# A gated linear-attention block: late division loads queued behind the second left side, first operands of the second layer asked for earlier

## The chip, the core and the metric

The kernel runs on one core of a Trainium2 chip. The metric is the device time of one execution in microseconds (us), as the median of several runs. The engines are named as in the profile: PE (matrix multiply), PEld (its weight loads), DVE (vector), ACT (scalar), POOL (GpSimd), SP (which here only issues transfers). POOL issues transfers too.

## What is computed

The reference, cut to what matters (S = 2048 tokens, D = 1024, F = 3584, 32 heads of 32, all float32):

```python
xn  = layernorm(x)
q, k, v = heads(xn @ wqkv)                    # phi(t) = where(t > 0, t + 1, exp(t)) + 1e-6
kv  = einsum("bhsd,bhse->bhde", phi(k), v);  z = sum over s of phi(k)
s   = (phi(q) @ kv) / (phi(q) . z + 1e-6) @ wo
g   = silu((silu(xn @ w1) * (xn @ w3)) @ w2)
out = x + s * g
```

## The kernel before, in words

Every large product is done by a Strassen-like scheme of seven products (`PRODUCTS`, L65: B11, T2, T3, T1, B21, T4, B22, each with its partner on the left: A11, S2, S3, S1, A12, A22, S4). Every operand is split into a high and a low part (`split`, L79: a cast on ACT at L83, then a subtraction on DVE at L84), and a product is three matmuls on those parts (`mm3`, L88: L91, L92, L93).

The first half of the program (two calls of `half`, L762) makes q, k, v and the gated hidden layer. Small side jobs run between its products: `catch_up` (L323) advances one job by one step and orders what the step issues behind marks, the copy and the addition just traced. The ordering call adds an order only between instructions of the same engine. A job that is queued with True is also ordered behind the load kept in the list `fetched` (L263), which is issued by SP; one queued with False is not.

Then comes **attention** (L967 to L973): eight groups of tokens, m = 0 to 7, 256 tokens each. The right side is the merged output weight: seven groups `wpr` of 1 MB each, loaded by two transfers each (L957) into two rotating `raw` buffers, split into tiles `wp` and kept for all tokens. The left side of a group of tokens is seven loads (`left`, L890) from `qs_d`, split into X tiles; those of m = 0 land in `job` buffers, the others in the four `sg` buffers. m = 0 is "outer": all seven products are built at once, step by step along the contraction (28 products of 3 matmuls), so that it can start while the right side is still coming. The others run one product after another, 84 matmuls each, with a `catch_up` after six of the seven.

`qs_d` is written by **divisions** (`divide`, L679): two loads of denominators (L688) and two of queries (L690), a multiplication on DVE (L696), four sums on POOL and a store (L699). There are four divisions for each m. Those for m = 6 and 7 are "late": the job of L764, whose steps run in the catch-ups of attention tokens 1 and on. It loads two divisions at its first step and one more after each finished one; a division has three empty steps before its multiplication. The `job` buffers are three.

The **second layer** (L974 to the end) multiplies the hidden layer by w2 in five segments; the first has 2 steps of contraction, the others 3. Its left side is again seven loads (L890, from `h_d` and `hs_d`), its right side `second_weights` (L905: a load at L907 into one of the six `c` buffers, which the attention's results s also use until they are stored), split into tiles of the pool `pw` (L974). `pw` takes the memory that the pools of the first part (`era1`: pa, praw, st, in that order, L100 to L102) give back at L973: its first tiles lie on the first of those pools, which is `pa`, where the attention's right side is. A tile waits for the tiles that lay at its addresses. In tracing order the second layer asks first for the left side of its tokens 0 (L984) and then for the right side (L985).

The program text gives the tracing order; a scheduler places the instructions on the engines' queues by that priority, by its own estimate of when each can run, and by free buffers. Each engine then works its queue in order.

Of the kernel before, what the change touches and what calls it, by code (L numbers as in the profile page):

```python
# [9 lines left out]
F32 = mybir.dt.float32  # L10
# [6 lines left out]
P = 128  # L17
C = 512
# [4 lines left out]
def tile_linear_attention_times_swiglu(  # L23
# [10 lines left out]
    nc = tc.nc  # L34
    x, out = x[0], out[0]
# [29 lines left out]
    PRODUCTS = ["B11", "T2", "T3", "T1", "B21", "T4", "B22"]  # L65
# [31 lines left out]
    pe = ctx.enter_context(tc.tile_pool(name="pe", bufs=3))  # L97
    pc = ctx.enter_context(tc.tile_pool(name="pc", bufs=6))
    era1 = ExitStack()
    pa = era1.enter_context(tc.tile_pool(name="pa", bufs=1))  # L100
    praw = era1.enter_context(tc.tile_pool(name="praw", bufs=2))
    st = era1.enter_context(tc.tile_pool(name="st", bufs=2))  # L102

    kvacc = st.tile([P, ND, P], F32, tag="kvacc", bufs=1, name="kvacc")
    nc.vector.memset(kvacc, 0.0)
# [1 line left out]
    def small(name):  # L107
        return pc.tile([P, C], F32, tag="c", name=name)

    def signed(name):  # L110
        return pc.tile([P, C], F32, tag="sg", bufs=4, name=name)

    def job_tile(shape, name):
        return praw.tile(shape, F32, tag="job", bufs=3, name=name)

    def load_rows(rows, name):

# [51 lines left out]
    def load_second(mom, g):  # L169

        ts = []
        for i in (2 * g, 2 * g + 1):
            ts.append(job_tile([P, D], f"xb{i}") if i < 3 else pb.tile([P, D], F32, tag="b", name=f"xb{i}"))
            nc.sync.dma_start(out=ts[-1], in_=x[C + i * P:C + (i + 1) * P, :])
        j = TH // 2 + 2 * g
        moments(ts, mom[:, j:j + 2])
        return ts
# [21 lines left out]
    def prepare_next(i):  # L199
# [12 lines left out]

        def steps(_):
            t = [job_tile([P, D], f"xn{i}_{e}") for e in range(2)]
            for c in range(2):
                r0 = HS + c * C + i * P
# [49 lines left out]
    fetched = []  # L266
# [54 lines left out]
    jobs = []  # L321
# [262 lines left out]
    def weight_sums(u, half):  # L584

        cols = slice(half * 2 * P, (half + 1) * 2 * P)

        def load():
            t = job_tile([P, 4, 2 * P], f"w2_{u}_{half}")
            for e in range(2):  # L590
                f = 2 * u + e
                nc.sync.dma_start(out=t[:, 2 * e:2 * e + 2],
                                  in_=w2[f * P:(f + 1) * P, :].rearrange("p (n c) -> p n c", c=C)[:, :, cols])
            return t

        def steps(t):
            yield True
            yield from sums_of(*(t[:, i] for i in range(4)))
            yield True
            nc.sync.dma_start(out=wt_d[u][:, :, cols], in_=t)  # L600
            yield True

        return Job(load, steps)
# [32 lines left out]
    def go_on(work):  # L636

        data = [j.load() for j in work[:2]]
        for i, j in enumerate(work):
            yield from j.steps(data[i])  # L640
            if i + 2 < len(work):
                data.append(work[i + 2].load())
# [36 lines left out]
    def divide(m, k):  # L679

        c, cols = m // NT, slice(m % NT * 2 * P, (m % NT + 1) * 2 * P)

        def load():
            t = job_tile([P, 4, 2 * P], f"qd{m}_{k}")
            for e in range(2):
                j = k + e * (ND // 2)
                rows = r_d[c][j * (P // DH):(j + 1) * (P // DH), cols]
                nc.sync.dma_start(out=t[:, 2 + e], in_=bass.AP(  # L688
                    tensor=rows.tensor, offset=rows.offset, ap=[[C, P // DH], [0, DH], [1, 2 * P]]))
                nc.sync.dma_start(out=t[:, e], in_=pq_d[j // JG][c][:, j % JG, cols])  # L690
            return t

        def steps(t):
            for _ in range(3):
                yield True
            nc.vector.scalar_tensor_tensor(t[:, :2], t[:, :2], 1e-6, t[:, 2:], op0=ALU.add, op1=ALU.mult)  # L696
            for _ in four_sums(t[:, 0], t[:, 1], t[:, 2], t[:, 3]):
                pass
            nc.gpsimd.dma_start(out=qs_d[m][:, k], in_=t)  # L699
            divided.add((m, k))  # L700
            yield True

        return Job(load, steps)
# [45 lines left out]
    def late_work():  # L749
        yield from go_on([divide(m, k) for m in range(LATE, S // (2 * P)) for k in range(ND // 2)])  # L750
# [10 lines left out]

    for h in range(NH):  # L762
        half(h)
    jobs.append((late_work(), False))  # L764


    GT = 2 * P
# [2 lines left out]
    class Segment:  # L770


        def __init__(self, name, nk, first, place, right, left, acc, end=None):
            self.name, self.nk, self.first = name, nk, first
            self.place, self.right_of, self.left_of, self.acc, self.end = place, right, left, acc, end
            self.Y, self.X = {}, {}
# [97 lines left out]
    def left(m, g, halves, sums, nk, name, first=False):  # L874

        halves = [t.rearrange("p k (g t s) -> p k g t s", t=2, s=P) for t in halves]
        sums = [t.rearrange("p k (n g s) -> p k n g s", n=2, s=P) for t in sums]
        where = {"A11": halves[0][:, :, g, 0], "A12": halves[1][:, :, g, 0], "A22": halves[1][:, :, g, 1]}
        for n in range(4):
            where[f"S{n + 1}"] = sums[n // 2][:, :, n % 2, g]  # L880
        big = None
        for e, n in enumerate(PRODUCTS):
            n = PARTNER[n]
            if first:
                if e % 2 == 0:
                    big = job_tile([P, 2, nk, P], f"r{e}{name}_{m}")
                t = big[:, e % 2]
            else:
                t = signed(f"r{n}{name}_{m}")[:, :nk * P].rearrange("p (k s) -> p k s", s=P)
            nc.sync.dma_start(out=t, in_=where[n])  # L890
            yield n, t

    def queries(m):
        while any((m, k) not in divided for k in range(ND // 2)):
            next(jobs[0][0])
        q = qs_d[m]
        return left(m, 0, [q[:, :, e] for e in range(2)], [q[:, :, 2 + e] for e in range(2)], ND // 2, "q", m == 0)

    def hiddens(i, m):
        h_ = h_d[i][m // NT].rearrange("p (k e) s -> p k e s", e=2)  # L900
        hs = hs_d[i][m // NT]
        return left(m, m % NT, [h_[:, :, e] for e in range(2)], [hs[:, :, e] for e in range(2)],
                    (FB[i][1] - FB[i][0]) // 2, f"B{i}")

    def second_weights(i, n, k):  # L905
        t = small(f"r{n}B{i}_{k}")
        nc.sync.dma_start(out=t, in_=second_weight(i, n, k))  # L907
        return t

    def second_weight(i, n, k):  # L910
        f0, f1 = FB[i]
        if n[0] == "T":
            return wt_d[f0 // 2 + k][:, ["T1", "T3", "T4", "T2"].index(n)]
        f = f0 + 2 * k + int(n[1]) - 1
        o = (int(n[2]) - 1) * C
        return w2[f * P:(f + 1) * P, o:o + C]
# [11 lines left out]
        nc.vector.tensor_add(a, a, xs)  # L928
        nc.gpsimd.dma_start(out=out[r0:r0 + P, cols], in_=a)

    def run(seg, nxt=None, around=None):

        def between(k):
            if m == NG - 1 and nxt:
                if k == 0:
                    nxt.operands(0)
                    for e in range(seg.nk, nxt.nk):
                        nxt.right(e)
                if k < nxt.nk:
                    nxt.right(k)  # L940

        if not seg.X:
            seg.operands(0)
        for m in range(NG):
            if m + 1 < NG:
                seg.operands(m + 1)
            seg.tokens(m, m == 0 or m == NG - 1 and nxt is not None, between)


# [11 lines left out]
    def attention_place(n, i, k):  # L961
# [3 lines left out]
    attention = Segment("s", ND // 2, True, attention_place,  # L965
                        attention_right, queries, lambda m, t, n: small(f"s{m}_{t}{n}"), store_s)
    attention.operands(0)  # L967
    for k in range(attention.nk):
        attention.right(k)
    run(attention)  # L970
    assert all(next(j, None) is None for j, _ in jobs)
    jobs.clear()
    era1.close()  # L973
# [2 lines left out]
    def layer_place(n, i, k):  # L976
        return pw.tile([P, 2, C], FR, tag=f"{n}_{k}", name=f"{n}_{k}")

    acc = []
    layers = [Segment(f"B{i}", (f1 - f0) // 2, i == 0, layer_place, lambda n, _, k, i=i: second_weights(i, n, k),  # L980
                      lambda m, i=i: hiddens(i, m), lambda m, t, n: acc[m][:, t, n],
                      finish if i == len(FB) - 1 else None)
              for i, (f0, f1) in enumerate(FB)]
    layers[0].operands(0)  # L984
    for k in range(layers[0].nk):  # L985
        layers[0].right(k)
    acc.extend(pw.tile([P, 2, 2, C], F32, tag=f"acc{m}", name=f"acc{m}") for m in range(NG))
    for i, seg in enumerate(layers):
# [24 lines left out]
```

## Time and profile before

| what | us |
|---|---|
| median of 3 runs | 2445.79 (2444.87 to 2446.43) |
| the profiled execution, its own time | 2438.58 |
| its span, first to last instruction | 2436.8 |
| PE busy | 2344.2 (96%) |
| DVE, ACT, POOL busy | 1810.3, 928.0, 723.7 |
| granted PE clock, mean | 0.992 |

The clock is given as a share of the full 2.4 GHz. A line of a timeline gives the start, the duration, the engine, the source line, the operation, what it writes and reads, how many instructions were merged, and in brackets how long the engine was idle before it and who released it.

### The profile page before, as it was taken

To read this page: it belongs to the slowest core of one execution; us is meant where nothing else is said; L and a number is where in the kernel's file an instruction comes from. 1 tells how busy PE (TensorE), PEld (TensorE's weight loads), DVE (VectorE), ACT (ScalarE), POOL (GpSimd) and SP (SyncE) were. 2 spreads that over 40 slices of the span, in tenths; PEclk is the share of its full clock that TensorE was granted. 3 is DMA by queue.
4 is the path that set the end of the run, shared out by engine and by line. 5 is a ranking of instruction groups with operands and counts; after the bars stand their busy time and mean duration, and the time that the engine had idled before them with its cause. 6 is when DMAs were issued, how large, how long until landed. Compare 5 with 4: busy or idle time off the path is not lost.

```text
span 2436.8 us, 30795 instructions
## 1 busy us (share of the span) xinstructions
PE 2344.2 (96%) x10544; PEld 1927.2 (79%) x10544; DVE 1810.3 (74%) x2688; ACT 928.0 (38%) x1663; POOL 723.7 (30%) x909
## 2 busy tenths in 40 slices
PE   6999989999999999999999999999899999999987
PEld 5788777778888888888778888888687887778776
DVE  8645788888887764657888887888655767776797
ACT  4434544332333233445433323333323434343443
POOL 3000021465554310000343543244330032323253
PEclk9999999999999999999999999999999999999999
DMA  4221555665555581124455556457776545454587
GB/s 139 70 69 45 172 168 171 220 212 196 184 203 178 184 290 35 52 83 144 163 192 180 191 191 207 136 187 243 242 234 194 152 130 157 120 163 116 169 288 240
DMA packets 375133, 408.62 MB, mean 168 GB/s; under 512 B 19840, under 2 KB 308608, under 8 KB 374976
## 3 DMA queue, kind: packets, MB, share of 16 engines
q1 hardware_dynamic: 348800, 319.35, 41.9%
q0 software_dynamic: 26176, 87.31, 9.5%
q8 instruction: 82, 1.34, 0.2%
q14 instruction: 75, 0.61, 0.1%
HBM read 268.96 MB, written 137.63 MB: 167 GB/s over the span
## 4 chain that ended last, share of the span: by engine, by line
PE 75%; DVE 11%; DMA 6%; issue 5%; ACT 1%; POOL 1%; SPq 0%; DVEq 0%; POOLq 0%; ACTq 0%
PE dB L93 1%; PE kv L442 1%; PE cB L91 1%; PE dB L91 1%; PE dB L92 1%; PE cB L93 1%; PE cB L92 1%; PE aB L93 1%; PE aB L91 1%; PE aB L92 1%; DMA wpr<-wp_d 1%; PE trk L409 1%; PE trv L409 1%; DMA rA11B<-h_d 1%; PE cs L93 1%
## 5 line engine op out<-in xcount | busy, mean ns | idle before, releaser
L511 POOL DMA_DIRECT2D pq_d<-pq x32 | 17.5, 548 | 501.2 <-DVE pq L403 461.6
L564 POOL DMA_DIRECT2D h_d<-sg x112 | 62.0, 553 | 331.1 <-DVE sg L563 320.6
L849 POOL TENSOR_TENSOR acc<-acc,uB 128x512 f32<-128x512 f32 x25 | 41.9, 1676 | 157.8 <-DVE uB L846 157.8
L546 POOL TENSOR_TENSOR qd<-qd 128x128 f32<-128x128 f32 x32 | 25.4, 795 | 129.1 <-DVE qd L696 121.1
L578 POOL TENSOR_TENSOR w<-w 128x256 f32<-128x256 f32 x28 | 26.4, 944 | 106.7 <-DMA w<-in_B_w 106.5
L826 POOL TENSOR_TENSOR acc<-acc,uB 128x512 f32<-128x512 f32 x7 | 10.9, 1560 | 149.3 <-ACT uB L818 149.3
L410 ACT ACTIVATE kvr<-trk 128x512 f32<-128x512 f32 x32 | 19.1, 597 | 88.0 <-PE trk L409 84.8
L550 POOL TENSOR_TENSOR hs<-sg,hs 128x256 f32<-128x256 f32 x56 | 51.9, 927 | 1.7
L547 POOL TENSOR_TENSOR hs<-hs,sg 128x256 f32<-128x256 f32 x56 | 46.5, 830 | 0.0
L919 POOL DMA_DIRECT2D s_d<-s x32 | 17.5, 546 | 92.9 <-DVE s L856 41.6
L546 POOL TENSOR_TENSOR hs<-sg,sg 128x256 f32<-128x256 f32 x56 | 42.1, 751 | 1.0
L91 PE MATMUL cB<-T,XA22B 128*128 128x512 f32 x87 | 35.0, 403 | 7.3 <-DVE acc L853 7.0
L549 POOL TENSOR_TENSOR hs<-sg 128x256 f32<-128x256 f32 x56 | 41.5, 740 | 0.0
L83 ACT CAST XS4B<-rS4B 128x384 fp32r<-128x384 f32 (+1 forms) x40 | 19.6, 490 | 54.0 <-PE cB L93 44.6
L851 POOL TENSOR_TENSOR acc<-acc,uB 128x512 f32<-128x512 f32 x25 | 40.0, 1600 | 0.0
L84 DVE TENSOR_TENSOR XS1B<-rS1B,XS1B 128x384 fp32r<-128x384 f32 (+1 forms) x40 | 36.4, 910 | 4.1 <-ACT XS1B L83 4.0
L867 DVE TENSOR_TENSOR acc<-cB,acc 128x512 f32<-128x512 f32 x25 | 17.2, 688 | 29.7 <-PE cB L93 29.7
L83 ACT CAST XS1B<-rS1B 128x384 fp32r<-128x384 f32 (+1 forms) x40 | 19.7, 493 | 48.5 <-PE cB L93 26.2
L926 ACT ACTIVATE acc<-acc 128x512 f32<-128x512 f32 x32 | 20.2, 632 | 46.3 <-DVE acc L856 14.1
L83 ACT CAST XA11B<-rA11B 128x384 fp32r<-128x384 f32 (+1 forms) x40 | 19.7, 493 | 44.9 <-PE dB L93 28.4
L83 ACT CAST XS3B<-rS3B 128x384 fp32r<-128x384 f32 (+1 forms) x40 | 19.7, 491 | 43.3 <-DMA rS3B<-hs_d 20.5
L91 PE MATMUL aB<-B,XA12B 128*128 128x512 f32 x87 | 34.1, 392 | 1.9 <-ACT uB L843 1.9
(5861 smaller groups left out, 8899.6 us busy)
## 6 DMA issues: line engine op xcount, KB each, us to landing
h_d<-sg POOLq DMA_DIRECT2D x112, 256.0 KB, 3.1
qs_d<-qd POOLq DMA_DIRECT2D x32, 512.0 KB, 4.1
hs_d<-hs POOLq DMA_DIRECT2D x60, 256.0 KB, 3.5
w<-in_B_w SPq DMA_DIRECT2D x56, 256.0 KB
wt_d<-w SPq DMA_DIRECT2D x28, 512.0 KB
hs_d<-hs SPq DMA_DIRECT2D x52, 256.0 KB
pq_d<-pq POOLq DMA_DIRECT2D x32, 256.0 KB, 3.0
pqd<-pq_d SPq DMA_DIRECT2D x16, 512.0 KB
```

Of the source, the lines that this page charges most:

```text
L83: nc.scalar.copy(out=hi, in_=src)
L91: nc.tensor.matmul(acc, lhsT=wh, rhs=ah, start=start, stop=False, skip_group_check=True)
L92: nc.tensor.matmul(acc, lhsT=wh, rhs=al, start=False, stop=False, skip_group_check=True)
L93: nc.tensor.matmul(acc, lhsT=wl, rhs=ah, start=False, stop=stop, skip_group_check=True)
L409: nc.tensor.transpose(p_[:, t * P:(t + 1) * P], src[:, t * P:(t + 1) * P], ident)
L546: nc.gpsimd.tensor_add(out=s1, in0=a21, in1=a22)
L547: nc.gpsimd.tensor_sub(out=s2, in0=s1, in1=a11)
L549: nc.gpsimd.tensor_sub(out=s3, in0=a11, in1=a21)
L550: nc.gpsimd.tensor_sub(out=s4, in0=a12, in1=s2)
L564: nc.gpsimd.dma_start(out=h_d[i][2 * h + c][:, 2 * k + n], in_=sg[n, c])
L849: G.tensor_add(out=c22, in0=c22, in1=u)
L851: G.tensor_add(out=c12, in0=c12, in1=u)
```

## The change

- The order in which the pools of the first part are opened is now st, pjob, praw, pa; the `job` buffers get a pool of their own (same number and size).
- The late divisions are queued with True, and `fetched` is set to the load just issued by `left` for attention tokens 0 and 1. So what SP issues for them in a catch-up is ordered behind the last left-side load of tokens 1.
- Ahead of the last attention tokens (m = 7), `ask_first` issues the loads of the second layer's B11, T2, T3 and T1 for contraction step 0, the first two into buffers of the pool `pe` (tag u, three buffers), the others into `c` buffers. `second_weights` uses them when it finds them.
- The first right side (k = 0) is traced ahead of the left side of tokens 0.

```diff
     era1 = ExitStack()
+    st = era1.enter_context(tc.tile_pool(name="st", bufs=2))
+    pjob = era1.enter_context(tc.tile_pool(name="pjob", bufs=3))
+    praw = era1.enter_context(tc.tile_pool(name="praw", bufs=2))
     pa = era1.enter_context(tc.tile_pool(name="pa", bufs=1))
-    praw = era1.enter_context(tc.tile_pool(name="praw", bufs=2))
-    st = era1.enter_context(tc.tile_pool(name="st", bufs=2))
...
-        return praw.tile(shape, F32, tag="job", bufs=3, name=name)
+        return pjob.tile(shape, F32, tag="job", name=name)
...
-    jobs.append((late_work(), False))
+    jobs.append((late_work(), True))
...
-            nc.sync.dma_start(out=t, in_=where[n])
+            load = nc.sync.dma_start(out=t, in_=where[n])
+            if name == "q" and m < 2:
+                fetched[:] = [load]
...
+    asked = {}
+    def ask(i, n, k, place):
+        asked[i, n, k] = t = place(f"r{n}B{i}_{k}")
+        nc.sync.dma_start(out=t, in_=second_weight(i, n, k))
     def second_weights(i, n, k):
-        t = small(f"r{n}B{i}_{k}")
-        nc.sync.dma_start(out=t, in_=second_weight(i, n, k))
-        return t
+        if (i, n, k) not in asked:
+            ask(i, n, k, small)
+        return asked[i, n, k]
+    def spare(name):
+        return pe.tile([P, C], F32, tag="u", name=name)
+    def ask_first():
+        for n, place in zip(PRODUCTS, (spare, spare, small, small)):
+            ask(0, n, 0, place)
...
             if m + 1 < NG:
                 seg.operands(m + 1)
+            elif ahead:
+                ahead()
...
-    run(attention)
+    run(attention, ahead=ask_first)
...
+    layers[0].right(0)
     layers[0].operands(0)
-    for k in range(layers[0].nk):
+    for k in range(1, layers[0].nk):
         layers[0].right(k)
```

## Rows read from the trace of the kernel before

**Rows 1.** The page, busy us of each engine, share of the span, instructions

```profile
PE 2344.2 (96%) x10544; PEld 1927.2 (79%) x10544; DVE 1810.3 (74%) x2688; ACT 928.0 (38%) x1663; POOL 723.7 (30%) x909
```

**Rows 2.** Stretches: us, busy (count) PE PEld DVE ACT POOL, clock, DMA share, GB/s

```profile
1704.90:1725.20 20.30, 11.91 (x31) 7.36 (x31) 10.21 (x15) 6.70 (x12) 6.13 (x9) 0.75 0.72 233
...
1745.20:1858.50 113.30, 113.30 (x501) 93.63 (x499) 55.23 (x85) 27.47 (x48) 32.20 (x59) 1.00 0.64 203
1858.50:1868.00 9.50, 5.52 (x13) 3.89 (x13) 5.16 (x8) 4.24 (x8) 0.54 (x1) 0.64 0.97 296
1868.00:1880.00 12.00, 12.00 (x53) 9.57 (x52) 9.53 (x17) 9.53 (x19) 0.00 (x0) 1.00 0.88 276
1880.00:1896.00 16.00, 14.54 (x59) 10.49 (x58) 15.59 (x32) 6.76 (x16) 0.00 (x0) 1.00 0.71 215
```

**Rows 3.** Who PE waited for: us in total, times, longest

```profile
PE T1s L91 <- ACT wp L83: 5.4, 1, 5.4
...
PE B11B L91 <- ACT B L83: 2.9, 1, 2.9
```

**Rows 4.** Timeline of SP, start of attention (merged issues)

```profile
1693.49 0.83 SPq L957 DMA_DIRECT2D wpr<-wp_d  x2
1694.69 0.57 SPq L688 DMA_DIRECT2D qd<-r_d  x1
...
1698.41 2.05 SPq L957 DMA_DIRECT2D wpr<-wp_d  x2
...
1707.50 0.53 SPq L688 DMA_DIRECT2D qd<-r_d  x1
1708.89 1.52 SPq L957 DMA_DIRECT2D wpr<-wp_d  x2
...
1728.38 0.52 SPq L890 DMA_DIRECT2D rS4q<-qs_d  x1
```

**Rows 5.** Transfers issued and moved from 1693 to 1721

```profile
DMA packets 5478, 8.46 MB, mean 302 GB/s; under 512 B 434, under 2 KB 4057, under 8 KB 5478
...
qd<-r_d SPq DMA_DIRECT2D x6, 128.0 KB
qd<-pq_d SPq DMA_DIRECT2D x6, 128.0 KB
```

**Rows 6.** Timelines of ACT, DVE and POOL, the right side's last groups

```profile
1699.27 1.14 ACT L83 CAST wp<-wpr 128x512 fp32r<-128x512 f32 x2 [1.45 <-DMA wpr<-wp_d]
...
1719.74 1.14 ACT L83 CAST wp<-wpr 128x512 fp32r<-128x512 f32 x2 [8.51 <-DMA wpr<-wp_d]
...
1699.93 4.39 DVE L84 TENSOR_TENSOR wp<-wpr,wp 128x512 fp32r<-128x512 f32 x2 [0.77 <-ACT wp L83]
...
1704.84 1.28 DVE L84 TENSOR_TENSOR wp<-wpr,wp 128x512 fp32r<-128x512 f32 x2
...
1700.01 0.75 POOL L546 TENSOR_TENSOR hs<-sg,sg 128x256 f32<-128x256 f32 x1
```

**Rows 7.** Timelines of DVE and SP, late divisions and last attention tokens

```profile
1737.36 0.69 DVE L696 SCALAR_TENSOR_TENSOR qd<-qd 128x512 f32<-128x512 f32 x1
...
1820.12 0.52 SPq L890 DMA_DIRECT2D rA11q<-qs_d  x1
...
1823.89 0.69 DVE L84 TENSOR_TENSOR XA11s<-rA11q,XA11s 128x512 fp32r<-128x512 f32 x1 [2.57 <-ACT XA11s L83]
...
1839.46 0.39 PE L91 MATMUL as<-wp,XA11s 128*128 128x512 f32 x1
```

**Rows 8.** Timelines of SP and ACT, start of the second layer

```profile
1857.03 0.52 SPq L890 DMA_DIRECT2D rS1B<-hs_d  x1
1857.64 0.55 SPq L907 DMA_DIRECT2D rB11B<-in_B_w  x1
...
1860.86 0.62 ACT L83 CAST B<-rB11B 128x512 fp32r<-128x512 f32 x1 [1.76 <-DMA rB11B<-in_B_w]
...
1867.88 0.62 ACT L83 CAST B<-rB22B 128x512 fp32r<-128x512 f32 x1 [0.83 <-DMA rB22B<-in_B_w]
```

More of the change, by code (lines that the diff above doesn't have):

```diff
@@ L929, in finish, with run @@
         nc.gpsimd.dma_start(out=out[r0:r0 + P, cols], in_=a)
-    def run(seg, nxt=None, around=None):
+    def run(seg, nxt=None, ahead=None):
         def between(k):
```

## The prediction

> **What bounds the kernel now.** I read the page first. PE is busy for 96% of the span, no other engine for more than 79% [rows 1]. So PE is the bound almost everywhere, and a change that leaves its 10,544 matmuls alone can only win where PE stands still or is fed late. The list of what PE waited for names two places with long single waits [rows 3]: 5.4 us before T1s, for a split of attention's right side, and 2.9 us before B11B, the second layer's first product. The stretches show both whole [rows 2]. From 1745.2 to 1858.5, inside attention, 501 matmuls took 113.3 us, which is 0.226 us each at full clock. Measured against that:
>
> - **Stall A**, the first attention tokens, 1704.9 to 1725.2: 31 matmuls are worth 7.0 us, and 20.3 passed. 13.3 us are lost. The granted clock is 0.75 on average: part of the stretch ran at the lower level of 1.2 GHz.
> - **Stall B**, the second layer's start: from 1858.5 to 1868, 13 matmuls are worth 2.9 of 9.5 us, so 6.6 are lost, at a mean clock of 0.64. From 1868 to 1880 PE is full. From 1880 to 1896, 59 matmuls are worth 13.3 of 16 us: 2.7 are lost, while DVE is busy 15.59 of 16. Together 9.3.
>
> The two stalls are all there is to win, 22.6 us at most.
>
> **What makes stall A.** PE waits for the last group of the right side. It is issued at 1708.89, and ACT can cast its first piece at 1719.74 [rows 4, 6], 10.9 us later; the group ahead of it is issued at 1698.41. In between the chip moves what it can: 8.46 MB from 1693 to 1721, at 302 GB/s [rows 5]. In that stretch SP issues twelve loads of 128 KB for three late divisions, from 1694.69 on, ahead of the last two groups and of the second tokens' left side [rows 4, 5]. Nobody needs them yet: the first late multiplication runs at 1737.36 [rows 7], at the catch-up where it was traced.
>
> **The change, part by part.**
>
> Queueing the late loads behind the second left side. Twelve loads of 131 kB are 1.57 MB, and at 302 GB/s they take 5.2 us out of the stretch ahead of the last group. SP's own order gives some back too: the buffer that the last group takes was last read at 1706.1 (the subtractions that start at 1704.84 and take 1.28), but the load is issued at 1708.89, behind the third division's loads, one of them at 1707.50 [rows 4, 6]. With bytes alone the first piece would come 5.2 us earlier, at 1714.5. Issued at 1706.1, and landing in 5.8 us as an earlier group did under the same traffic (issued at 1693.49, cast at 1699.27 [rows 4, 6]), it would come at 1711.9. I take 1713, 6.7 us earlier. From that cast to the end of the twelve remaining matmuls 5.5 us pass now; twelve at full clock are 2.7, and the last ones ran slower because PE had stood still for 5.4 us. A shorter stop saves about 1 us of that. **Term A: 6.7 + 1 = 7.7 us**; its bounds are 0, if other transfers take the room, and 13.3, the whole stall.
>
> One rule bears on how far the issue of that group can move up. The two subtractions at 1699.93 take 4.39 us where a pair takes 1.28 at 1704.84, and POOL's sums of the hidden layer start at 1700.01 [rows 6]; the change moves neither. The Trainium skill, page "SBUF — State Buffer", section "SBUF: two separate sides", says that the port pair shared by VectorE and GpSimd is locked for a whole instruction, while transfers use other ports; by it the slow pair is POOL's doing and stays, and the trace agrees with its 4.39. If the crowded transfers had slowed the pair instead, it would shrink by 3.1 us and term A would be about 10 us.
>
> What is moved must go somewhere. The twelve issues, some 0.56 us each or 6.7 us of SP, now stand behind the last left-side load of tokens 1 (at 1728.38 before [rows 4], at about 1721 after), beside the loads for tokens 2. Those are needed 19 us after tokens 1 began (84 matmuls of 0.226), so they have some 15 us of room. The first division's data must be there for the multiplication, at 1737.4 - 7.7 = 1729.7: its four loads leave from 1721 to 1724 and have about 5 us to land. Later divisions wait for a freed buffer now as before. I cost this at nothing; the cover is those 5 us, and after them the four of eight accumulator banks that the running tokens leave free, 2.7 us of PE each.
>
> Asking early for four operands of the second layer. Today B11B's load is issued at 1857.64, on SP right behind a left-side load of tokens 1 at 1857.03 [rows 8], although that weight was ready in DRAM long before. Its cast starts at 1860.86, that of B22 at 1867.88: seven products in 7 us. (The times here are without the shift by term A.) With B11, T2, T3 and T1 loaded and split during the last tokens, PE starts at 1858.5 with 12 matmuls (2.7 us, to 1861.2). B21, T4 and B22 then stand first in the queue instead of fifth: at worst the first is cast where B11 is now, 1860.86, and the others follow one subtraction (0.69) apart. So PE gets through contraction step 0 by about 1863.5 and through step 1 at the pace of the splits, three matmuls (0.68) for each. Of the 6.6 us I leave 1.5. Of the 2.7 behind it I take nothing: DVE still has the next segment's splits there. **Term B: 5 us**, bounds 0 and 9.3. Nothing below: four loads are moved, none added, and the stretch around 1850 moves 203 GB/s on average, well under 302.
>
> The pools' order makes those splits possible. The first seven tiles of `pw` are 28 KB for each partition; st, pjob and praw hold about 8 + 12 + 16 = 36 KB, all unread once the last division is stored. Before, they lay on the right side that the last tokens still read. The two borrowed u buffers leave one for the tokens: u of m = 7 is written after its first product, 2.7 us after m = 6 ended, and the last read of u before it takes 0.69. Nothing waits there.
>
> **The sum.** 7.7 + 5 = 12.7 us. The profiled execution took 2438.58, which becomes 2425.9. Its time lies 7.2 below the median of 2445.79; taking the same off the median gives **2433.1**. A difference of about 0.2%, 4.9 us, is what a measurement of this kernel can tell from no change.
>
> **The rivals.**
>
> *Only stall A goes.* The buffers and memory let the four splits run no earlier, or the three unasked operands come late and hold PE as B11 does now. Speaks for it: B11B's load came late although some `c` buffer must have been free; what held it in the queue the rows don't show. Against: the four have their own buffers, and the memory is free. 7.7 us: 2438.1. Chance 0.13.
>
> *Only stall B goes.* Attention's start is full of transfers anyway: stores of POOL and the second left side fill the room of the late loads, and the last group lands as late. For: 302 GB/s over the stretch. Against: less is asked for before that group. 5 us: 2440.8. Chance 0.09.
>
> *Slower: the late divisions become late.* Their place is the multiplication on DVE and, behind it, the left side of tokens 7, whose first load leaves at 1820.12. Its split ends at 1824.6 and PE wants it at 1839.46 [rows 7], so there are 14.9 us of slack. If every division moved as far as its first load does, from 1694.69 to 1728.38 or 33.7 us, PE would stand 18.8 us before tokens 7, against 12.7 won: 6.1 slower, 2451.9. It decides once the chain of divisions moves by more than 14.9 + 12.7 = 27.6 us. Against: their pace is that of the catch-ups, and the first multiplication comes 42.7 us after its first load. Chance 0.06.
>
> *Nothing worth measuring.* The scheduler's queues come out otherwise than the text suggests, and PE finds other waits of the same size: within 4 us of 2445.8. Chance 0.10.
>
> **How the numbers follow.** Both stalls shrinking has 0.62. Its own gain lies between 7 and 18 us, since each term can be off by half. The range reaches from 18.3 us won, short of the cap of 22.6, to 4.3 won, which takes in the rival with stall B alone: 2427.5 to 2441.5; left out are the last two rivals and the tails. Faster by over 0.2%: 0.60 of the forecast, 0.11 of the first rival, 0.05 of the second, in all 0.76. Slower 0.06. The same, 0.18.
>
> **What would show it right or wrong.** On SP: no load of L688 or L690 between the groups of the right side, twelve of them right behind the last left-side load of tokens 1. The last group is cast at about 1713, PE's wait before T1s falls from 5.4 to 2 or less, and the clock over the stretch rises. The first late multiplication stays close behind the product where it stands, with an idle time before it of under 2 us. At the second layer's start: four casts of weights before the last attention product, no wait of 2.9 us before B11B, and a clock near 1.00 where it was 0.64. I am wrong on A if the last group still lands about 10 us after its issue, and on B if PE waits as long for B21 as it did for B11. A wait of PE before tokens 6 or 7 would be the third rival.

## The result and the profile after

The changed kernel takes 2456.56 us (median of 4 runs, 2455.28 to 2459.99) against 2445.33 for the kernel before on the same chip: ratio 1.0049, 95% interval 1.0037 to 1.0061. It is **slower by 11.2 us**; 2433.1 was predicted. The profiled execution of after is the highest of its four (2459.99), the one of before lay 7 below its median, so the two profiles differ by 21.4, and some 10 us of that are the executions'. Stages are therefore compared by their lengths, and whole kernels by medians.

The page's busy times of after:

```profile
PE 2366.6 (96%) x10544; PEld 1933.4 (79%) x10544; DVE 1812.4 (74%) x2688; ACT 926.8 (38%) x1663; POOL 722.4 (29%) x909
```

The same 10,544 matmuls keep PE busy for 22.4 us longer than in [rows 1], while the other engines stay where they were. A wait would not show there: PE itself works longer. (Executions differ in this too: the kernels below with the spacing of before have PE busy for 2344.2 to 2353.1 us, those with the spacing of after for 2366.0 to 2368.9.) Next, three full stretches (first half, second half, second layer) by busy time (count) of PE, PEld, DVE, ACT and POOL, clock, DMA share and GB/s. Before:

```profile
740.00:880.00 140.00, 140.00 (x619) 115.91 (x619) 103.65 (x130) 42.75 (x72) 53.46 (x76) 1.00 0.64 223
1300.00:1500.00 200.00, 200.00 (x884) 165.60 (x883) 160.87 (x204) 61.81 (x105) 95.87 (x145) 1.00 0.58 193
1950.00:2050.00 100.00, 100.00 (x443) 82.81 (x442) 67.05 (x106) 33.51 (x66) 32.22 (x22) 1.00 0.41 120
```

After:

```profile
740.00:880.00 140.00, 140.00 (x614) 114.86 (x613) 101.64 (x130) 42.10 (x71) 54.10 (x74) 1.00 0.58 198
1300.00:1500.00 200.00, 200.00 (x875) 164.07 (x874) 162.90 (x206) 64.76 (x111) 91.04 (x133) 1.00 0.56 188
1950.00:2050.00 100.00, 100.00 (x443) 82.81 (x442) 71.66 (x115) 37.95 (x74) 28.19 (x19) 1.00 0.48 142
```

PE is full and at full clock in all six. Yet 200 us hold 884 matmuls before and 875 after, hundreds of microseconds ahead of the first instruction that the change reorders; the second layer, 443 and 443, is untouched. In the trace the starts of matmuls are 226 or 227 ns apart before, 226.67 on average, and in after's first layer between 226 and 232, 228.95 on average. The products' three lines hold 7,440 matmuls up to the end of attention, and all but the 48 that merge the output weight read the tiles of the pool `pa`: 7,392 x 2.28 ns = 16.9 us.

The two stalls, by the same view of after (the answers to [rows 2]):

```profile
1720.00:1740.70 20.70, 18.68 (x71) 13.44 (x70) 19.47 (x22) 8.96 (x16) 9.28 (x14) 0.92 0.87 274
1760.80:1880.40 119.60, 119.60 (x523) 98.06 (x522) 59.62 (x93) 31.15 (x55) 36.47 (x67) 1.00 0.68 218
1880.40:1890.00 9.60, 6.99 (x27) 4.56 (x26) 5.63 (x10) 3.28 (x7) 0.54 (x1) 1.00 0.88 257
1890.00:1902.00 12.00, 12.00 (x52) 9.28 (x52) 11.27 (x21) 9.60 (x21) 0.00 (x0) 1.00 0.86 269
1902.00:1918.00 16.00, 13.03 (x50) 9.88 (x49) 13.41 (x27) 5.07 (x12) 0.00 (x0) 0.89 0.63 189
```

Attention's start holds 71 matmuls in 20.7 us where it held 31 in 20.3. The second layer's first 9.6 us hold 27 instead of 13, at clock 1.00 instead of 0.64; but its third stretch now falls to 50 in 16 us. PE's list of waits says the same. T1s is gone from it, and so are the 2.9 us before the second layer's first product [rows 3]; the 1.3 that the list still has before a B11B belong to the second step of the contraction. The two longest of the new waits, and that one:

```profile
PE cs L91 <- DVE s L855: 3.2, 1, 3.2
...
PE cB L91 <- ACT XS3B L83: 2.8, 1, 2.8
...
PE B11B L91 <- ACT B L83: 1.3, 1, 1.3
```

**Start of attention.** SP of after (answers to [rows 4]), then ACT's first cast of the last group [rows 6]:

```profile
1718.01 13.17 SPq L978 DMA_DIRECT2D wpr<-wp_d  x6
...
1742.74 0.62 SPq L892 DMA_DIRECT2D rS4q<-qs_d  x1
1743.42 0.56 SPq L690 DMA_DIRECT2D qd<-r_d  x1
...
1748.03 0.56 SPq L690 DMA_DIRECT2D qd<-r_d  x1
1748.64 0.54 SPq L692 DMA_DIRECT2D qd<-pq_d  x1
1749.27 0.54 SPq L892 DMA_DIRECT2D rS3q<-qs_d  x1
```

```profile
1735.24 1.14 ACT L83 CAST wp<-wpr 128x512 fp32r<-128x512 f32 x2 [4.21 <-DMA wpr<-wp_d]
```

The groups of the right side go out in one piece, and the late loads begin behind rS4q, the last left-side load of tokens 1. Then they alternate with the left side of tokens 2: six of the twelve stand ahead of its rS3q. That load leaves 8.6 us after the first product of tokens 1, where it left 7.0 after it before, and it also takes longer: before, it was issued at 1732.18 and cast 4.2 us later, in after 6.8 us later (from 1749.27). ACT before, then after:

```profile
1736.34 0.62 ACT L83 CAST XS3s<-rS3q 128x512 fp32r<-128x512 f32 x1 [0.30 <-DMA rS3q<-qs_d]
```

```profile
1756.05 0.62 ACT L83 CAST XS3s<-rS3q 128x512 fp32r<-128x512 f32 x1 [3.15 <-DMA rS3q<-qs_d]
```

What that costs stands on DVE, and on PE behind it:

```profile
1756.70 0.69 DVE L84 TENSOR_TENSOR XS3s<-rS3q,XS3s 128x512 fp32r<-128x512 f32 x1 [3.07 <-ACT XS3s L83]
1757.31 0.68 DVE L855 TENSOR_TENSOR s<-cs,us 128x512 f32<-128x512 f32 x1
```

```profile
1758.04 0.66 PE L91 MATMUL cs<-wp,XA22s 128*128 128x512 f32 x1 [3.20 <-DVE s L855]
```

DVE stands 3.07 us before a split of tokens 2; the addition behind it, which empties an accumulator bank for tokens 1, is late, and PE waits 3.20 for it. The matmul after the wait takes 0.66 instead of 0.39 us, and the eight behind it start 0.43 us apart instead of 0.23, at a mean clock of 0.62 from 1757.5 to 1762. That is another 1.6 us; with the wait, 4.8.

**Start of the second layer.** ACT of after (answers to [rows 8]):

```profile
1878.41 0.62 ACT L83 CAST B<-rB11B 128x512 fp32r<-128x512 f32 x1
...
1882.75 0.62 ACT L83 CAST B<-rB21B 128x512 fp32r<-128x512 f32 x1 [1.50 <-DMA rB21B<-in_B_w]
...
1889.10 0.62 ACT L83 CAST B<-rB11B 128x512 fp32r<-128x512 f32 x1 [3.29 <-DMA rB11B<-in_B_w]
...
1907.95 0.40 ACT L83 CAST XS3B<-rS3B 128x256 fp32r<-128x256 f32 x1 [2.80 <-DMA rS3B<-hs_d]
```

The first B11B is cast at 1878.41, 2 us ahead of attention's last matmul (1880.38). The lateness has moved on: to the B11B of step 1 and then to a left-side operand, rS3B, which SP issues at 1900.78 behind weights of the next segment.

Three marks by their distances carry the rest. A: the last product of the hidden layer to the first of tokens 1, 31.6 us before. M: from there to the end of attention, 133.1 before. B: from there to the first product of the second segment, 74.3 before.

| kernel | A | M | B | won by the three, before rounding | won by medians |
|---|---|---|---|---|---|
| after | 23.3 | 139.7 | 73.6 | 2.4 | -11.2 |
| e1, order of after, right side elsewhere | 22.8 | 138.1 | 70.3 | 7.7 | 7.5 |
| e2, order of after, 448 bytes more ahead of `pa` | 22.8 | 138.5 | 73.3 | 4.5 | 6.5 |
| e5, loads reordered alone | 22.4 | 138.8 | 74.9 | 2.8 | 2.8 |
| e6, operands asked early alone | 31.7 | 133.1 | 69.8 | 4.3 | 4.0 |
| e7, late loads one token later | 22.1 | 141.7 | 70.5 | 4.6 | 2.9 |
| e11, late loads spread | 22.1 | 135.1 | 71.0 | 10.8 | 10.1 |

Each row of stages is one execution. e9 and e16, which keep the order of the kernel before, have 30.2 and 31.9 for A, 133.1 and 133.4 for M, 73.9 and 74.9 for B, so a stage is known to about 1.5 us. In after, 1.3 us of M are the spacing of its 588 matmuls (e3, e4, e8 and e10, with that spacing and the old order, have 134.4 to 134.7). Where the first layer's matmuls keep their spacing (all but after), the three stages give the whole difference within some 2 us. In after they don't; 13.6 us are missing, and they lie in the spacing.

### The profile page after: what moved, and what is told of

Read it like the earlier page. It is cut to its first block, busy times and chain, and to the rows that moved or that the text cites. A ratio compares the mean times of both kernels' runs of the same rounds, so it can differ in the third digit from the quotient of the medians.

```text
span 2458.2 us, 30793 instructions
## 1 busy us (share of the span) xinstructions
PE 2366.6 (96%) x10544; PEld 1933.4 (79%) x10544; DVE 1812.4 (74%) x2688; ACT 926.8 (38%) x1663; POOL 722.4 (29%) x909
## 4 chain that ended last, share of the span: by engine, by line
PE 72%; DVE 10%; issue 7%; DMA 6%; POOL 2%; ACT 2%; SPq 0%; DVEq 0%; POOLq 0%; ACTq 0%
PE cB L91 1%; PE kv L444 1%; PE cB L93 1%; PE dB L92 1%; PE dB L91 1%; PE cB L92 1%; PE dB L93 1%; PE aB L91 1%; PE aB L93 1%; PE aB L92 1%; PE den L666 1%; DMA rS1B<-hs_d 1%; PE trk L411 1%; PE trv L411 1%; DVE sg L565 1%
## 5 line engine op out<-in xcount | busy, mean ns | idle before, releaser
L91 PE MATMUL cB<-T,XS3B 128*128 128x512 f32 x87 | 34.3, 394 | 2.8 <-ACT XS3B L83 2.8
L444 PEld LDWEIGHTS kv<-kvr 128*128 128x128 f32 x256 | 34.1, 194 | 2.6
```

What stands on the lines that cost most here:

```text
L91: nc.tensor.matmul(acc, lhsT=wh, rhs=ah, start=start, stop=False, skip_group_check=True)
L444: nc.tensor.matmul(acc, lhsT=r[:, 1, t], rhs=r[:, 0, t], start=t == 0, stop=t == C // P - 1)
```

## The experiments

**Where the right side lies: e1 to e4.** The pools lie one behind another in each partition. In the kernel before, as built, the stationary operands (pool pb; `lhsT` of a matmul, 128x128) start at byte 17,600 and `pa`, the moving operands of the first layer and of attention (`rhs`, 128x512), at 76,992. In the changed order st, pjob and praw come first, and `pa` starts 36,416 bytes higher, at 113,408. e1 opens `st` behind `pa` and leaves the rest of after as it is, with the same order of instructions on every engine; `pa` then starts 28,672 bytes (112 x 256) above its place in the kernel before. e2 keeps the pools' order and adds 448 bytes ahead of `pa`, which makes it 36,864 (144 x 256). e3 and e4 are the kernel before with the new pool order alone, and with 64 unused bytes ahead of `pa`.

```diff
 # e1
-    st = era1.enter_context(tc.tile_pool(name="st", bufs=2))
     pjob = era1.enter_context(tc.tile_pool(name="pjob", bufs=3))
     praw = era1.enter_context(tc.tile_pool(name="praw", bufs=2))
     pa = era1.enter_context(tc.tile_pool(name="pa", bufs=1))
+    st = era1.enter_context(tc.tile_pool(name="st", bufs=2))
 # e4 (e2: [P, 112], with the pools of after)
+    pad = era1.enter_context(tc.tile_pool(name="pad", bufs=1)).tile([P, 16], F32, name="pad")
+    nc.vector.memset(pad, 0.0)
     pa = era1.enter_context(tc.tile_pool(name="pa", bufs=1))
 # e3
+    st = era1.enter_context(tc.tile_pool(name="st", bufs=2))
+    pjob = era1.enter_context(tc.tile_pool(name="pjob", bufs=3))
+    praw = era1.enter_context(tc.tile_pool(name="praw", bufs=2))
     pa = era1.enter_context(tc.tile_pool(name="pa", bufs=1))
-    praw = era1.enter_context(tc.tile_pool(name="praw", bufs=2))
-    st = era1.enter_context(tc.tile_pool(name="st", bufs=2))
...
-        return praw.tile(shape, F32, tag="job", bufs=3, name=name)
+        return pjob.tile(shape, F32, tag="job", name=name)
```

> The changed kernel with the pool st opened last of the first part's pools (pjob, praw, pa, st): every engine's instructions and their order stay as in the changed kernel, only addresses differ. Theory 'address': the changed kernel's matmuls on tiles of pa run at 0.2286 us apart where before they ran at 0.2262, because pa's start moved from 192 to 256 (modulo 512 bytes); here it is at 192 again, so the spacing between 740 and 880 us is 0.2262 again, and the time falls by some 15 us against the changed kernel, to 2436 to 2442. Rival 'order': the slow matmuls come from the new order of loads or from the run, and the time stays above 2450 with a spacing near 0.2286.

> The changed kernel with 448 unused bytes ahead of pa, so that pa starts at 192 modulo 512 again; pools in the changed order. Theory 'address': spacing 0.2262 and a time within 3 us of the kernel with st last. Rival 'order': spacing near 0.2286 and above 2450.

> The kernel before with the changed order of pools and nothing else of the change. Theory 'address': 6,300 or more matmuls times 2.3 ns, 14 to 20 us slower than before, 2459 to 2465, spacing 0.2286. Rival 'order' (the slowness belongs to the late loads or the early asks): same as before within 3 us.

> The kernel before with 64 unused bytes ahead of pa, so that pa starts at 256 modulo 512 as in the changed kernel, with the old order of pools and of loads. Theory 'address' in its low bits: 14 to 20 us slower than before, spacing 0.2286. If only a larger part of the address matters (pa lies 36 KB lower here than in the changed kernel): same as before within 3 us.

Measured beside 2444.71 for the kernel before: e1 2437.21 (0.9972, 0.9963 to 0.9982), e2 2438.18 (0.9976, 0.9966 to 0.9985), e3 2459.78 (1.0063, 1.0050 to 1.0076), e4 2459.5 (1.0059, 1.0047 to 1.0072). The second half's full stretch, e1 and then e3:

```profile
1300.00:1500.00 200.00, 200.00 (x884) 165.66 (x883) 162.72 (x209) 61.82 (x105) 92.65 (x140) 1.00 0.57 191
```

```profile
1300.00:1500.00 200.00, 200.00 (x875) 164.04 (x874) 162.71 (x205) 64.72 (x112) 91.02 (x133) 1.00 0.56 189
```

The same instructions with the right side elsewhere are 884 instead of 875, and 64 unused bytes cost the kernel before 14.8 us. So the place of `pa` makes the loss (between after and e2 only `pa` has moved), and without it the change wins 6.5 to 7.5 us.

**The parts of the change alone: e5 to e7.** e5 is the kernel before with only the ordering of the late loads, e6 is e1 without it, e7 is e1 with the loads behind tokens 2 instead of tokens 1.

```diff
 # e5, on the kernel before
-    jobs.append((late_work(), False))
+    jobs.append((late_work(), True))
...
-            nc.sync.dma_start(out=t, in_=where[n])
+            load = nc.sync.dma_start(out=t, in_=where[n])
+            if name == "q" and m < 2:
+                fetched[:] = [load]
 # e6, on e1
-    jobs.append((late_work(), True))
+    jobs.append((late_work(), False))
 # e7, on e1
-            if name == "q" and m < 2:
+            if name == "q" and m < 3:
```

> The kernel before with the late loads queued behind the second left side, and nothing else of the change (old pools, no early asks). Theory 'moved loads': the right side's last group is cast some 8 us earlier, so attention's tokens 1 start about 22.8 us after the last product of the hidden layer instead of 31.6, but the twelve loads now stand among the left side of tokens 2, and some 5 us go again between the start of tokens 1 and the end of attention; net 3 to 5 us faster than before, 2440 to 2442. Rival 'cheap move' (the 5 us belong to the early asks or the pools): 8 us faster, about 2437, no wait of PE for L853 in tokens 1.

> The changed kernel with st last (pa at its old place modulo 512), without the ordering of the late loads: only the early asks, the tracing order of the first right side and the pools. Theory 'small B': 2 to 4 us faster than before, 2441 to 2443; the first wait of the second layer is gone, part of it comes back in its tokens 1 and 2; attention's start as before (31.6 us from the last hidden product to tokens 1). Rival 'asks do nothing' once pa lies right: same as before within 1 us.

> The changed kernel with st last, and the late loads ordered behind the left side of tokens 2 instead of tokens 1. Theory 'displaced left side': the 3 us wait of PE in tokens 1 (DVE stands before the split of S3 of tokens 2) goes, and the time falls by up to 5 us against the kernel with st last, to 2432 to 2435. Rival 'late divisions': the first multiplication L698 now comes before its data and DVE stands there instead, so the time is the same as with st last or higher, 2437 to 2445.

Measured beside 2444.29: e5 2441.46 (0.9985, 0.9976 to 0.9994), e6 2440.32 (0.9983, 0.9974 to 0.9993), e7 2441.36 (0.9983, 0.9974 to 0.9991). PE's waits of e5, then of e6:

```profile
PE cs L91 <- DVE s L853: 4.0, 1, 4.0
PE B11B L91 <- ACT B L83: 2.9, 1, 2.9
```

```profile
PE T1s L91 <- ACT wp L83: 5.4, 1, 5.4
```

Each part takes away the wait it is about. The ordering brings the new wait of 3 to 4 us before cs, and asking early brings none of that. The two gains, 2.8 and 4.0, add up to 6.8; e1 has 7.5, which is the same within the intervals. In e7, the first late multiplication does come before its data, as its rival said, and DVE stands there:

```profile
1746.10 0.69 DVE L698 SCALAR_TENSOR_TENSOR qd<-qd 128x512 f32<-128x512 f32 x1 [6.30 <-DMA qd<-pq_d]
```

PE's new wait has another source, though:

```profile
PE as L91 <- ACT us L845: 5.8, 1, 5.8
```

```profile
1754.77 0.62 ACT L83 CAST XA11s<-rA11q 128x512 fp32r<-128x512 f32 x1 [12.51 <-DMA rA11q<-qs_d]
1758.00 0.62 ACT L83 CAST XS2s<-rS2q 128x512 fp32r<-128x512 f32 x1 [2.61 <-DMA rS2q<-qs_d]
1758.52 0.58 ACT L845 COPY us<-as 128x512 f32<-128x512 f32 x1
```

The copy that PE waits for stands on ACT behind two casts of the left side of tokens 3, and the first of these stood 12.51 us for its load. SP issued that load at 1747.41, right behind the twelve. In both places that were tried, behind tokens 1 and behind tokens 2, the heap of twelve loads makes the next left side late. That DVE's stand of 6.30 us cost PE anything, the list of waits does not show.

**Which places must agree: e8 to e10 and e12.** e8 is e4 with 320 bytes. e9 has 64 bytes more in the pool of constants, so that all pools move together; e10 has these and 64 more ahead of `pa`. e12 has 64 bytes behind the stationary operands and 64 more ahead of `pa`, so that the scratch pools and the second layer's right side move by 64 and `pa` by 128.

```diff
 # e9 and e10
+    cpad = const.tile([P, 16], F32, name="cpad"); nc.vector.memset(cpad, 0.0)
     zacc = const.tile([P, ND], F32, name="zacc")
 # e12
     pb = ctx.enter_context(tc.tile_pool(name="pb", bufs=8))
+    gap = ctx.enter_context(tc.tile_pool(name="gap", bufs=1)).tile([P, 16], F32, name="gap")
+    nc.vector.memset(gap, 0.0)
     pe = ctx.enter_context(tc.tile_pool(name="pe", bufs=3))
 # e10 and e12, ahead of pa: the 64 bytes of e4; e8: [P, 80]
```

> The kernel before with 320 unused bytes ahead of pa, so that pa starts at 0 modulo 512. If a start at an odd multiple of 64 bytes is what keeps the spacing at 0.2267 us, this is slow like the 64-byte pad (about 2459); if what counts is that pa and the pool of the left operands start at the same place modulo 512, it is slow too; if only 256 modulo 512 is bad, it is the same as before, 2445; a better start than 192 would show in a spacing under 0.2267 and a time under 2440.

> The kernel before with one unused tile of 64 bytes per partition more in the pool of constants: every pool behind it (left operands, scratch, right operands of both layers) starts 64 bytes higher, all at multiples of 128. Nothing else changes. Theory (absolute: a matmul whose moving operand starts at a multiple of 128 bytes is slower, wherever the left operand lies): the spacing in the full stretches becomes 228.9 ns instead of 226.7 in the first layer and in the second one too. The first layer loses the 15 us that the two shifted pools cost; from the end of attention on, 564 us at 226.7 ns are some 2,490 matmuls, which lose another 5.5 us: about 2465. Rival (relative: it is the distance between left and right operand that counts): both moved together, spacing 226.7 ns, 2445.

> The same, and 64 unused bytes more ahead of the first layer's right side, which therefore starts 64 bytes above a multiple of 128 as in the kernel before, while the left operands, the scratch and the second layer's right side start at multiples of 128. Theory (absolute): 226.7 ns between matmuls in the first layer, 228.9 in the second: about 2450. Rival (relative): 228.9 ns in the first layer, 226.7 in the second: about 2460. If the two stalls of the start were at issue and not the spacing, neither would move: 2445.

> The kernel before with 64 unused bytes behind the left operands and 64 more ahead of the first layer's right side. The left operands and the first layer's right side stand as before in their place modulo 128, the scratch and the second layer's right side are moved by 64 bytes. Theory (what counts is the place of the moving operand against that of the stationary one, the left operands): 226.7 ns between matmuls in the first layer as before, and 228.9 in the second, which only here is out of step with the left side: some 5.5 us, about 2450. Rival (what counts is the place of the moving operand against the scratch that ScalarE and VectorE read and write beside it): 228.9 ns in the first layer, 226.7 in the second: about 2460. If neither pair decides: 2445.

Measured: e8 2460.04 (1.0060, 1.0048 to 1.0073), e9 2444.1 (1.0004, 0.9995 to 1.0013), e10 2459.62 (1.0064, 1.0052 to 1.0077), e12 2479.06 (1.0139, 1.0122 to 1.0156). e9 and e10 end the theory that I had put first, that the moving operand's own place decides: moved together with the stationary one it costs nothing, and left where it was modulo 128, while the other has moved, it costs 15 us. 320 bytes off (e8) is as slow as 64. e12 came out slower than either of its theories had it. The second layer is at 228.9 ns, as the pair of stationary and moving operands wants it, but the first is slower than in any run before:

```profile
1300.00:1500.00 200.00, 200.00 (x863) 162.08 (x862) 160.01 (x202) 62.70 (x108) 87.61 (x127) 1.00 0.55 188
1950.00:2050.00 100.00, 100.00 (x438) 82.04 (x438) 71.84 (x125) 39.08 (x80) 20.67 (x13) 1.00 0.48 140
```

Its `pa` was 128 bytes off the stationary operands. That is the same place modulo 128, but not modulo 256.

**The distance: e13 to e16.** The kernel before with 32, 128, 192 and 256 bytes ahead of `pa` (the diff of e4 with [P, 8], [P, 32], [P, 48] and [P, 64]).

> The kernel before with 32 unused bytes ahead of the first layer's right side, which then lies 32 bytes off the place of the left operands modulo 512; nothing else moves. Theory (the spacing of matmuls grows with the distance between moving and stationary operand, as far as 64 and 128 bytes show it: 228.9 and 232.4 ns): between 226.7 and 228.9 ns in the first layer, about 227.8, some 7 us, 2452. Rival (only whole pieces of 64 bytes count): 226.7 and 2445, or, if a start inside such a piece makes each read touch two of them, as slow as 64 bytes off or slower, 2460 and more. Second layer 226.7 in each case.

> The same with 128 bytes: the right side of the first layer is in the same place modulo 128 as in the kernel before, and 128 bytes off modulo 512; scratch and second layer stay. Theory (distance between moving and stationary operand, not their place modulo 128): 232.4 ns in the first layer as in the run with the two gaps, 226.7 in the second; that run's 2479.1 less what its second layer lost, which is 0.4 us by its marks and 5.5 by its spacing: 2474 to 2479. Rival (the place modulo 128, with the scratch as the third party of the run with the two gaps): nothing is out of step here, 226.7 ns and 2445.

> The same with 192 bytes. Theory (distance, repeating after 256 bytes, since 64 and 320 off gave the same 228.9): a value of its own, not one of those that are known; if the pattern is symmetric, 192 off is 64 short of the next repeat and gives 228.9 ns, 2460; if it grows by some 3 ns for each 64, about 236 ns and 2500. Rival (place modulo 128): the same as 64 off in every respect, 2460 with intervals of 226, 229 and 232 ns.

> The same with 256 bytes. Theory (distance, repeating after 256): 226.7 ns and 2445. Rival (it repeats after 512 only): slower than 228.9 ns, above 2460, and the equality of 64 and 320 bytes off is a chance one.

The second half's full stretch with 32, 128, 192 and 256 bytes, one kernel each:

```profile
1300.00:1500.00 200.00, 199.01 (x853) 159.93 (x854) 158.27 (x201) 62.96 (x109) 87.40 (x126) 1.00 0.56 187
```

```profile
1300.00:1500.00 200.00, 200.00 (x862) 162.11 (x861) 159.22 (x201) 62.65 (x108) 87.33 (x126) 1.00 0.56 188
```

```profile
1300.00:1500.00 200.00, 200.00 (x859) 161.19 (x858) 159.14 (x201) 62.66 (x108) 85.10 (x125) 1.00 0.55 187
```

```profile
1300.00:1500.00 200.00, 200.00 (x884) 165.62 (x883) 163.38 (x210) 61.21 (x104) 91.21 (x138) 1.00 0.57 193
```

The runs in order of the distance from pb to `pa` modulo 256 bytes, with the mean spacing of matmuls in that stretch (e5, e6, e7 and e11 lie at 0 too, with 226.67):

| distance | kernels | spacing, ns | time against before |
|---|---|---|---|
| 0 | before, e9, e16 (256 bytes) | 226.67 | 1, 1.0004, 1.0007 (0.9995 to 1.0018) |
| 0 | e1, e2, with the change's order | 226.67 | 0.9972, 0.9976 |
| 64 | e3, e4, e8 (320 bytes), e10 | 228.9 to 229.0 | 1.0063, 1.0059, 1.0060, 1.0064 |
| 64 | after | 228.95 | 1.0049 |
| 128 | e14, e12 | 232.4 | 1.0145 (1.0128 to 1.0162), 1.0139 |
| 192 | e15 | 233.3 | 1.0163 (1.0148 to 1.0178) |
| 32 | e13 | 233.3 | 1.0165 (1.0150 to 1.0180) |

The time follows the distance, repeating after 256 bytes, whatever lies between. e14 has the scratch where it is in the kernel before and is as slow as e12, so the scratch has no part. The values at 32 and 192 were not foreseen: 32 bytes off are among the worst, and the pattern is not symmetric. Both rest on one kernel each.

**A version that beats both: e11.** e1, with the late divisions asked for one ahead instead of two and each load behind the newest left side.

```diff
-    fetched = []
+    fetched, newest = [], []
...
-    def go_on(work):
+    def go_on(work, n=2):
-        data = [j.load() for j in work[:2]]
+        data = [j.load() for j in work[:n]]
-            if i + 2 < len(work):
-                data.append(work[i + 2].load())
+            if i + n < len(work):
+                data.append(work[i + n].load())
...
+            if m >= LATE:
+                fetched[:] = newest
...
-        yield from go_on([divide(m, k) for m in range(LATE, S // (2 * P)) for k in range(ND // 2)])
+        yield from go_on([divide(m, k) for m in range(LATE, S // (2 * P)) for k in range(ND // 2)], 1)
...
-            if name == "q" and m < 2:
-                fetched[:] = [load]
+            if name == "q":
+                newest[:] = [load]
+                if m < 2:
+                    fetched[:] = [load]
```

> The version with the pools in the order job tiles, raw tiles, attention, state (2437.2), with the late divisions asked for one ahead instead of two, each behind the newest left side of a token tile. So four loads of 128 KB, not twelve, stand on SP between the left sides of tokens 2 and 3. Theory (the 5 us that the moved loads cost between the first tokens' start and the end of attention are the loads of tokens 2 landing late among the twelve): the wait of DVE before the split of tokens 2 and PE's wait of 3.1 us behind it go, the stretch from the first product of tokens 1 to the end of attention takes 133 to 135 us instead of 138.1, total 2432 to 2435. Rival (the late divisions are then late themselves): DVE stands before a multiplication of a late division for 3 us or more, PE waits behind it, stretch 138 or longer, total 2437 or above.

2434.69 beside 2444.81 for the kernel before: 0.9960, 0.9947 to 0.9972, the fastest of all. PE's waits and SP:

```profile
PE cs L91 <- DVE s L857: 1.1, 1, 1.1
```

```profile
1727.53 0.47 SPq L692 DMA_DIRECT2D qd<-pq_d  x1
1728.10 0.54 SPq L894 DMA_DIRECT2D rS2q<-qs_d  x1
1729.34 0.52 SPq L894 DMA_DIRECT2D rS3q<-qs_d  x1
...
1735.92 0.56 SPq L690 DMA_DIRECT2D qd<-r_d  x1
```

rS3q of tokens 2 leaves with four late loads ahead of it and none for 6.6 us behind it. It leaves no earlier than in e1 (8.25 us after the first product of tokens 1, against 7.92), but it is cast 4.6 us after its issue instead of 7.0. PE's wait of 3.1 falls to 1.1, and stage M to 135.1, just above the 133 to 135 expected. So some 3 of the 5 us that the moved loads cost in e1 came from the left side of tokens 2 landing late among them.

## Why the prediction was wrong

**The step that failed** is the pools' order, "The pools' order makes those splits possible", a paragraph without a term in the sum. It even adds up "st, pjob and praw hold about 8 + 12 + 16 = 36 KB", but asks only whether there is room. Those 36,416 bytes are 142 x 256 + 64: they put the moving operands of the whole first layer 64 bytes out of step with the stationary ones. By e3, e4, e8 and e10 that costs 14.8 to 15.8 us; between after (1.0049) and e1 (0.9972), with the same instructions, it is 0.8%, some 19 us. None of the rivals held it. The premise behind it is in the first paragraph, that a change which leaves the 10,544 matmuls alone can only act where PE stands still: it takes the pace of 0.226 us as given, and the pace is what changed. No row could have given the price, since the operands of all the large products in the kernel before are in step; but a moved buffer is a change, and the text should have bounded it rather than passed over it. Nor were the two stalls "all there is to win": PE's full list of waits before has longer single ones, 11.2 us before tA at the program's start and 6.0 before bg in the first layer, which the change does not touch.

**Term A was right**: 7.7 predicted, 8.8 measured in e1 and 8.3 in after. In after the last group's first cast comes 17.8 us after the last hidden product (1735.24 less 1717.42) instead of 26.1 (1719.74 less 1693.60), 8.3 earlier where I took 6.7: the group's load was issued at 1730.39, which is 2.3 us earlier by the same mark, and it was cast 4.9 us after its issue instead of 10.9. The clock over the stretch rose from 0.75 to 0.92. The slow pair of subtractions beside POOL's sums [rows 6] stayed: 4.38 us in after, 3.85 in e1.

```profile
1724.18 4.38 DVE L84 TENSOR_TENSOR wp<-wpr,wp 128x512 fp32r<-128x512 f32 x2 [0.79 <-ACT wp L83]
```

This agrees with the sentence that the prediction took from the Trainium skill's page "SBUF — State Buffer", section "SBUF: two separate sides". The other reading, about 10 us, needed the pair to shrink by 3.1.

**Moving the late loads was costed at nothing, and costs 5.0 us** (stage M of e1). The named cover, 5 us for the first division and four banks, did cover the divisions: their multiplication does not wait at tokens 1. What I said of tokens 2, "some 15 us of room", is where it failed. Twelve loads among the seven use that room up: rS3q left 1.6 us later and took 2.6 us longer to be cast, and DVE's fixed order passes the lateness from a split of tokens 2 to an addition of tokens 1, which PE needs much earlier than the split. The forecast's third rival looked for late divisions; at tokens 1 they were on time, and even in e7, where the first one was not, PE's wait came through a left side.

**Term B was nearly right where its stage held**: 5 predicted, 4.4 by stage and 4.0 by medians in e6, 4.0 by stage in e1, but 0.7 in after's one profile and 1.0 in e2's. B11 and its three companions are cast while attention's last product runs, and the clock over the first stretch stays at 1.00. There 27 matmuls are worth 6.1 of 9.6 us, so 3.5 are still lost where I left 1.5. What after and e2 lose again lies behind that: in the third stretch their clock is 0.89, with waits for left-side operands (XS3B 2.8 in after, XA12B 1.3 and XS3B 1.1 in e2), while e1 keeps its pace:

```profile
1881.50:1897.50 16.00, 14.59 (x64) 11.42 (x63) 15.31 (x32) 7.28 (x17) 0.00 (x0) 1.00 0.66 203
```

after and e2 share the changed order of pools, which e1, e6, e7 and e11 do not have. Whether that order costs these 3 us or the executions differ by them is open; the medians of e1 and e2 differ by 1.0.

So the sum of what I priced, less the 5 us that I priced at nothing, is 7.7 - 5 + 5 = 7.7, and e1 won 7.5. That this fits so well is partly luck: by e1's stages term A was 1.1 too small and term B 1.0 too large. The whole of the wrong sign is the place in memory.

## What to carry to other kernels

An edit that moves a buffer can change the time of every matmul that reads it: where the matmuls are like these (128x128 by 128x512, fp32), keep moving and stationary operands a multiple of 256 bytes apart, and after a change of pools or sizes compare the number of matmuls in a full stretch far from the edit before reading any wait. A load is not free because nobody waits for it soon: ask which urgent load stands behind it on its queue or lands beside it, and spread the moved ones instead of queuing them in one heap. To judge an edit of order, run it once with the memory layout held fixed.

## What was not expected of the hardware

With the same instructions, full PE and clock 1.00, fp32 matmuls of 128x128 by 128x512 follow each other every 226.67 ns when moving and stationary operand start a multiple of 256 bytes apart in their partition, 228.95 ns at 64 bytes off, 232.4 at 128 and 233.3 at 32 and 192. The last of these, over the first layer and attention, is 1.6% of the kernel. The place itself, away from the distance, made no difference in the one kernel that moved both (e9). Why the distance matters was not tried; the weight loads beside the matmuls take 187 to 188 ns on average in each of these stretches (PEld's busy time by its count), so they show no sign of it.
